# A new step order for fused attention and expert layer, with banks and memory of their own for the last steps of attention

## The chip, the cores and the metric

The kernel runs on one core of one Trainium2 chip. The metric is the device time of one execution in microseconds. Engines are named as in the profile: PE (TensorE, the matrix engine; PEld are its weight loads), ACT (ScalarE), DVE (VectorE), POOL (GpSimd) and SP (SyncE, which only issues transfers). Each engine works through its own instructions in the order in which they were written, and waits on semaphores for the others.

## The reference

Causal attention over 4 batches, 12 heads, 448 positions, 64 wide, and behind it a mixture of 8 experts over the 1792 tokens, each of which goes to one expert:

```python
scores = scale * np.matmul(q, k.transpose(0, 1, 3, 2))       # causal mask, then softmax
attn = np.exp(scores - max); attn = attn / (sum + 1e-09)
x = (attn @ v).transpose(0, 2, 1, 3).reshape(1792, 768)
xn, en = x / (norm(x) + 1e-06), expert_emb / (norm(expert_emb) + 1e-06)
logits = xn @ en.T / tau                                     # (1792, 8)
expert_idx = argmax(logits); gate_w = softmax(logits)[expert_idx]
out[mask] = gate_w * (maximum(x[mask] @ w1[e], 0) @ w2[e])   # w1: 768x1024, w2: 1024x768 per expert
```

## The kernel before

Attention goes by pairs of heads, 24 in all (`NP`), each cut into 4 chunks of 112 query rows. The steps of a pair `p` have short names, and the string `ORDER` (lines 36 to 103) says in which order the steps are issued, `name.pair` by `name.pair`; every instruction of a step joins its engine's queue at that place. The steps the text uses:

- `LD` loads q, k and v of a pair (SP, two transfers, to 4 buffers in turn). `EE` loads the experts' embedding.
- `S0` to `S3` (line 348, PE): the scores of chunk i, 112(i+1) columns, of both heads at once, one head to a bank each. `sp_ring` has two pairs of banks and hands them out in turn: the third score step must wait until the first has been read.
- `Mih` (line 358, DVE) masks the scores of chunk i, head h, and takes the row maximum; `Eih` (line 362, ACT) is the exponential with the row sum.
- `T0`, `T1`, `T20`, `T21`, `T30`, `T31` (line 373, PE) transpose the probabilities by the groups of `GROUPS`, into two banks in turn (`pt_ring`), and `V..` (line 381) copies them out, on ACT ("A") or DVE ("V").
- `PV0` to `PV3` (line 390, PE) are the products with v into the bank `bo`; `VO` (ACT) copies them out. `SA` (POOL) and `RC` (DVE) make the reciprocal of the sums; `X` (PE) and `XE` (DVE) turn and scale the result into rows of x; `WX` writes x to memory.
- Every third pair: `LT` (PE) makes expert logits in the bank `bx`, `LS` (ACT) copies them, `LO` (PE) turns them, `LE` (DVE) scales them. At the end of a batch `R0` to `Rc` choose the expert and rank the tokens (DVE, with `RK` on PE), and `Q0` to `Q3` (ACT) square the rows of x.
- `es0` to `esA`, once: the norm of the experts' embedding. `es1` is a square root on ACT.
- After three batches `Z0` to `Z5` find the most used expert so far, the star. `LW`, `W`, `Wl` load its w1, round it and keep the rest of the rounding (SP, ACT, POOL); `LL`, `Ak`, `Bk` do so with w2 (SP, ACT, DVE), k being one of 8 blocks.
- The end: `XT`, `XH`, `XL` turn and split the first tile of 128 gathered tokens; `F0` to `F5` (PE, line 633) are its product with w1, `RL` (ACT) copies the result, `HT`, `HH`, `HL` turn and split it, `G0` to `G5` are the first six of the eight blocks of its product with w2. `N0` to `Nc` (DVE) and `TB` (PE) make the table of which token goes to which tile, `GA` (POOL) gathers tile 1, `xt`, `xh`, `xl` turn and split it.

Behind `ORDER` come the tiles of the expert layer (`body`, line 822): each has two products (line 633), weights that are loaded when the expert changes, and a scattered write to the output.

Memory is reused: `after` (line 159) gives a buffer a second tile of another type when the first is done with in full. So `aq` (line 175) holds the loaded q and k (`raws`) and the probabilities (`Ps`), and its second tile `aqr` holds the split of the first tile and parts of w2, and may be written only when the last probability has been read. `ar` holds the mask and the logits, and after them `h2[0]`, block 0 of w2.

```python
raws = ring_of(4, P, 2, S, src=aq)                       # line 193
h2 = Parts([part(rr, 0, 0, DM)] + ...)                   # line 221: block 0 of w2 follows the mask and the logits
xh_ring = Ring(part(qr, 0, 0, KD, P), ...)               # line 225
```

Before the first step PE turns the identity 24 times (line 793).

Of the kernel before, what the change touches and what calls it, by code (L numbers as in the profile page):

```python
# [40 lines left out]
PV3.0 E00.2 S2.2 LD.4 SA.1 VO.0 RC.1 S3.2 M20.2 E01.2 E10.2 M21.2 T30.1 E11.2 M30.2 T20.1 E20.2 M31.2 X.0 V30.1 V20.1
S0.3 S1.3 E21.2 XE.0 T21.1 E30.2 T31.1 M00.3 V21.1 E31.2 V31.1 T30.2 E00.3 M01.3 SA.2 T20.2 V30.2 M10.3 S2.3 M11.3 E01.3
V20.2 S3.3 E10.3 M20.3 E11.3 M21.3 PV0.1 E20.3 M30.3 E21.3 M31.3 PV1.1 E30.3 PV2.1 RC.2 PV3.1 E31.3 T0.2 LD.5 T21.2 VO.1
SA.3 S0.4 V21.2 V0.2 S1.4 M00.4 M01.4 T1.2 RC.3 E00.4 T31.2 E01.4 M10.4 X.1 V1.2 M11.4 V31.2 S2.4 E10.4 XE.1 S3.4 E11.4
M20.4 PV0.2 M21.4 E20.4 M30.4 PV1.2 E21.4 M31.4 PV2.2 E30.4 PV3.2 T30.3 LD.6 VO.2 T20.3 E31.4 X.2 V20.3 V30.3 S0.5 XE.2
SA.4 S1.5 T0.3 RC.4 T21.3 V0.3 M00.5 LT.2 M01.5 V21.3 E00.5 E01.5 T1.3 LS.2 T31.3 V1.3 M10.5 LO.2 M11.5 E10.5 T30.4
V31.3 E11.5 S2.5 LE0.2 LE1.2 V30.4 LE2.2 S3.5 M20.5 M21.5 E20.5 PV0.3 M30.5 E21.5 M31.5 PV1.3 E30.5 PV2.3 E31.5 PV3.3
T20.4 LD.7 VO.3 T0.4 V20.4 SA.5 S0.6 V0.4 S1.6 RC.5 M00.6 M01.6 T21.4 E00.6 T1.4 V21.4 E01.6 X.3 V1.4 M10.6 T31.4 M11.6
T30.5 E10.6 XE.3 E11.6 S2.6 V31.4 V30.5 S3.6 M20.6 M21.6 PV0.4 E20.6 M30.6 E21.6 PV1.4 M31.6 E30.6 PV2.4 PV3.4 E31.6
T20.5 LD.8 T0.5 VO.4 V20.5 S0.7 SA.6 V0.5 S1.7 RC.6 M00.7 T21.5 M01.7 E00.7 T1.5 V21.5 E01.7 X.4 V1.5 M10.7 T31.5 M11.7  # L50
E10.7 T30.6 XE.4 E11.7 S2.7 V31.5 V30.6 S3.7 M20.7 M21.7 PV0.5 E20.7 M30.7 E21.7 PV1.5 M31.7 E30.7 PV2.5 PV3.5 E31.7
T20.6 LD.9 T0.6 VO.5 V20.6 SA.7 S0.8 V0.6 S1.8 RC.7 M00.8 M01.8 LT.5 E00.8 E01.8 T21.6 LS.5 T1.6 V21.6 X.5 V1.6 M10.8
T31.6 M11.8 T30.7 E10.8 XE.5 E11.8 S2.8 V31.6 V30.7 WX.5 S3.8 M20.8 Q0.5 M21.8 LO.5 Q1.5 M30.8 T20.7 T0.7 LE0.5 LE1.5
PV0.6 V0.7 LE2.5 V20.7 Q2.5 PV1.6 R0.5 Q3.5 PV2.6 M31.8 PV3.6 R1.5 T21.7 LD.10 VO.6 R2.5 T1.7 V21.7 E20.8 X.6 R3.5 V1.7
T31.7 R4.5 XE.6 E21.8 S0.9 S1.9 R5.5 E30.8 V31.7 T20.8 RK.5 E31.8 R8.5 T30.8 V20.8 PV0.7 R6.5 SA.8 V30.8 R9.5 R7.5 M00.9
# [912 lines left out]
```

## Time and profile before

| | |
|---|---|
| median of 3 runs | 540.91 us (539.68 to 540.98) |
| the profiled execution | 539.1 us, its span (first to last instruction) 537.4 us |
| PE busy in the span | 505.7 us, 94% |
| ACT, DVE, POOL busy | 327.9, 315.2, 70.4 us |
| mean granted clock of PE | 0.97 |

The columns of the profile's views: the timeline has the start from the span's start, the time until the last of the merged instructions ends, engine, line, operation and tiles, the count, and in brackets the idle time before and who ended it. Instructions of one engine overlap a little, so what one costs in a row of equal ones is the distance of their starts, not their duration. The view by windows has, for each stretch, every engine's busy time and count, the granted clock of PE (1.00 is 2.4 GHz, 0.50 is 1.2 GHz), the share of the DMA engines and GB/s.

### The profile page before, as it was taken

The numbers are of one execution on the slowest core, as the hardware profiler recorded it, in microseconds if no ns is written. First come the engines' busy times: TensorE is split into PE (matmuls) and PEld (weight loads), VectorE is DVE, ScalarE is ACT, GpSimd is POOL, SyncE is SP. The second block draws the span as 40 slices with busy tenths as digits, with TensorE's granted clock in tenths as the row PEclk, the third lists the DMA queues.
The fourth block names the chain that finished last, engine by engine and source line by source line (L and its number), as shares of the span: only waits on it lengthen the run. The fifth ranks groups of instructions, "written<-read, shape, count | busy, mean of one in ns | idle before, by whom it ended". The sixth has DMA issues, their size and how long they took to land. (4 is left out here: it accounts for less than half of the span.)

```text
span 537.4 us, 10476 instructions
## 1 busy us (share of the span) xinstructions
PE 505.7 (94%) x3184; PEld 405.3 (75%) x3184; DVE 315.2 (59%) x872; ACT 327.9 (61%) x775; POOL 70.4 (13%) x90
## 2 busy tenths in 40 slices
PE   5899999999999959579999999999999999999994
PEld 4465666665666547568989989998899889988984
DVE  0686787778768827733014698181949362073962
ACT  2998889888988869122125587162939352164861
POOL 2000000000000650023011102121110211010111
PEclk9799999999999979779999999999999999999998
DMA  8032263345226933030153965729495700739551
GB/s 236 7 103 69 91 204 104 105 122 169 72 72 205 362 137 104 1 89 30 60 221 116 404 233 185 263 65 383 166 393 184 267 31 30 295 133 390 177 176 35
DMA packets 27364, 87.16 MB, mean 162 GB/s; under 512 B 2694, under 2 KB 3142, under 8 KB 27280
## 3 DMA queue, kind: packets, MB, share of 16 engines
q1 hardware_dynamic: 24160, 72.38, 38.4%
q0 software_dynamic: 3120, 13.77, 7.3%
q8 instruction: 39, 0.64, 0.5%
q14 instruction: 45, 0.37, 0.2%
HBM read 144.33 MB, written 12.58 MB: 292 GB/s over the span
## 5 line engine op out<-in xcount | busy, mean ns | idle before, releaser
L364 ACT ACTIVATE aq<-aq,mx 112x112 f32<-112x112 f32 (+1 forms) x192 | 99.6, 522 | 10.3 <-DVE mx L359 10.2
L359 DVE CUSTOM_DVE_ANT_0 aq<-bank,ar 112x112 f32<-112x112 f32 (+1 forms) x192 | 76.6, 444 | 16.7 <-PE bank L355 14.0
L379 PE MATMUL bank<-idt,aq 112*112 112x112 f32 x480 | 65.1, 271 | 12.4 <-ACT aq L364 6.4
L379 PEld LDWEIGHTS bank<-idt,aq 112*112 112x112 f32 x480 | 47.7, 136 | 32.2 <-ACT aq L364 14.5
L355 PE MATMUL bank<-aq 64*112 64x112 f32 (+3 forms) x384 | 60.1, 428 | 0.1
L384 DVE COPY ap<-bank 112x336 f32<-112x336 f32 (+1 forms) x72 | 38.9, 543 | 33.5 <-PE bank L379 27.9
L820 DVE TENSOR_TENSOR wl<-fa,wh 128x1024 fp32r<-128x1024 f32 x42 | 48.5, 1223 | 13.2 <-PE bank L638 10.8
L392 PE MATMUL bank<-ap 112*64 112x448 f32 (+3 forms) x384 | 51.8, 409 | 0.0
L662 ACT COPY fa<-bank 128x512 f32<-128x512 f32 x28 | 15.2, 588 | 59.9 <-PE bank L637 51.8
L392 PEld LDWEIGHTS bank<-ap 112*64 112x64 f32 x384 | 26.1, 137 | 29.9 <-issue 19.4
L819 ACT CAST wh<-fa 128x1024 fp32r<-128x1024 f32 x42 | 40.8, 1048 | 11.8 <-PE bank L639 9.6
L703 POOL DMA_INDIRECT out_dram<-fa,isx x18 | 25.1, 1395 | 168.7 <-ACTq L830 40.0
L355 PEld LDWEIGHTS bank<-aq 64*112 64x112 f32 x384 | 27.9, 176 | 12.5 <-issue 0.9
L384 ACT COPY ap<-bank 112x448 f32<-112x448 f32 (+1 forms) x72 | 33.3, 466 | 5.5 <-PE bank L379 5.1
L364 ACT ACTIVATION_READ_ACCUMULATOR aq<-aq,mx 112x1 f32 x192 | 36.5, 190 | 0.0
L543 POOL DMA_INDIRECT fa<-xd,ig x21 | 20.7, 986 | 111.6 <-PE bank L595 78.5
L637 PE MATMUL bank<-wh,aor 128*128 128x512 f32 x84 | 33.8, 402 | 0.0
L638 PE MATMUL bank<-wl,aor 128*128 128x512 f32 x84 | 33.6, 400 | 0.0
L639 PE MATMUL bank<-wh,apr 128*128 128x512 f32 x84 | 33.6, 399 | 0.0
L637 PE MATMUL bank<-wh,aqr 128*128 128x512 f32 x84 | 32.9, 392 | 0.0
L639 PE MATMUL bank<-wh,aqr 128*128 128x512 f32 x84 | 32.8, 391 | 0.0
L638 PE MATMUL bank<-wl,aqr 128*128 128x512 f32 x84 | 32.8, 390 | 0.0
(267 smaller groups left out, 1064.8 us busy)
## 6 DMA issues: line engine op xcount, KB each, us to landing
fa<-in_w_dram SPq DMA_DIRECT2D x76, 768.0 KB
fa<-in_w_dram SPq DMA_DIRECT2D x54, 1024.0 KB
aq<-in_qk_dram SPq DMA_DIRECT2D x24, 448.0 KB
ap<-in_vv_dram SPq DMA_DIRECT2D x24, 224.0 KB
xd<-fa SPq DMA_DIRECT2D x3, 1344.0 KB
fa<-in_w_dram SPq DMA_DIRECT2D x6, 512.0 KB
xd<-fa SPq DMA_DIRECT2D x1, 1120.0 KB
fa<-xd,ig POOLq DMA_INDIRECT x21, 4.7
```

The source lines that it names most:

```text
L355: pe.matmul(sp[h][:CP, :n], raws[p % 4][rows, 0, CP * i : CP * i + CP], raws[p % 4][rows, 1, :n], start=True, stop=True, tile_position=(D ...
L359: v.tensor_tensor_reduce(out=Ps[p % 2][i, h], in0=st.pop(("sp", p, i, h)), in1=mask[i], scale=-0.125, scalar=3e38, op0=ALU.add, op1=ALU.mi ...
L364: ac.activation(x, x, AF.Exp, bias=mxs[p % 3][:, h, i : i + 1], scale=-1.0, accum_out=sums[p % 3][:, h, i : i + 1])
L379: pe.transpose(t[:, x, c], Ps[p % 2][i, h][:, c * CP : c * CP + CP], idt[:CP, :CP])
L384: (ac.copy if q == "A" else v.tensor_copy)(o, st.pop(("pt", p, n)))
L392: pe.matmul(bo[64 * h : 64 * h + 64, CP * c : S], vts[p % 4][:, c, 64 * h : 64 * h + 64], PTs[p % 2][:, h, 4 * c : 3 * c + NC], start=c == ...
L637: pe.matmul(acc[j], xh[:, k], wh[k][:, o], start=k == 0, stop=False)
L638: pe.matmul(acc[j], xh[:, k], wl[k][:, o], start=False, stop=False)
L639: pe.matmul(acc[j], xl[:, k], wh[k][:, o], start=False, stop=k == nk - 1)
L703: g.indirect_dma_start(out=out, out_offset=IndirectOffsetOnAxis(ap=isx[:, t : t + 1], axis=0), in_=ob, in_offset=None, bounds_check=N - 1, ...
L819: ac.copy(h[k], r[:, k])
L820: v.tensor_tensor(l[k], r[:, k], h[k], op=ALU.subtract)
```

## The change

- `ORDER` is another order throughout. The scores of chunks 0 and 2 are now one step (`S02`, 448 columns in one pair of banks), so that a pair takes three turns of `sp_ring`, not four: `S02`, `S3`, `S1`. `es0` stands behind the first exponentials, where it stood ahead of them.
- `T20` and `T21` are copied out by ACT instead of DVE.
- `es1` takes the square root on DVE, 12 small instructions, instead of ACT.
- `end_ring`, the two banks of the second pair of `sp_ring`, serves `XT`, the last `LO`, the last `RK`, `HT` and `TB`; the last `LT` goes to `bo`. Before, the first, fourth and fifth went to `pt_ring`, and the logits and the ranking to `bx`.
- `raws` have a buffer `ak` of their own; the split of the first tile and the blocks 1 and 2 of w2 follow them there.
- Block 0 of w2 comes last for the first tile (`K0`), so that `ORDER` has `G1` to `G6`.
- 16 turns of the identity instead of 24.

```diff
@@ a line of ORDER's first and last part
-LD.0 LD.1 LD.2 EE.0 LD.3 es0.0 es1.0 S0.0 S1.0 M00.0 M01.0 M10.0 S2.0 M11.0 E00.0 S3.0 es2.0 E01.0 M20.0 E10.0 M21.0
+LD.0 LD.1 S02.0 EE.0 LD.2 S3.0 M01.0 M21.0 E01.0 M00.0 M20.0 E21.0 M30.0 S1.0 LD.3 E00.0 M31.0 E20.0 T21.0 T0.0 M11.0
-F4.23 Q3.23 A7.23 F5.23 B7.23 LT.23 RL0.23 RL1.23 HTa.23 LS.23 HTb.23 LO.23 LE0.23 LE1.23 LE2.23 R0.23 R1.23 R2.23 R3.23
+A3.23 X.23 XLb.23 LS.23 F0.23 XE.23 A4.23 B3.23 WX2.23 LO.23 A5.23 F1.23 B4.23 A6.23 LE2.23 LE0.23 A7.23 LE1.23 F2.23
...
+K0 = [1, 2, 3, 4, 5, 6, 7, 0]
-GROUPS = {"0": ((0, 1), 0, "A"), "1": ((0, 1), 1, "A"), "20": ((0,), 2, "V"), "21": ((1,), 2, "V"),
+GROUPS = {"0": ((0, 1), 0, "A"), "1": ((0, 1), 1, "A"), "20": ((0,), 2, "A"), "21": ((1,), 2, "A"),
...
+        end_ring = Ring(*bank[2:4])
...
-        aq, qr = after("aq", 4 * 2 * S + 4 * TRI)
+        ak, kr = after("ak", 4 * 2 * S)
+        aq, qr = after("aq", 5 * DM + F)
...
-        step("es1", FIRST)(lambda p: ac.activation(es[:, 2:3], es[:, 0:1], AF.Sqrt))
+            v.tensor_scalar(guess, es[:, 0:1].bitcast(I32), 1, None, ALU.arith_shift_right)
+            v.tensor_scalar(guess, guess, 532487669.0, None, ALU.add)
+            for _ in range(2):
+                for f in newton(es[:, 2:3], es[:, 0:1], es[:, 2:3], es[:, 3:4]):
+                    f()
...
+            for i in chunks:
+                n = CP * (i + 1)
+                for h in range(2):
+                    st["sp", p, i, h] = o = sp[h][:CP, at : at + n]
+                    pe.matmul(o, raws[p % 4][rows, 0, CP * i : CP * i + CP], raws[p % 4][rows, 1, :n],
+                              start=True, stop=True, tile_position=(D * h, 0), skip_group_check=len(chunks) > 1)
+                at += n
...
+            st["lt"] = bo if p == NP - 1 else bx
+            st["lo"] = t = cut(end_ring.next() if p == NP - 1 else bx, CP, NC, 96)
+            rk = rks[p] = cut(end_ring.next() if p == NP - 1 else bx, CP, NC + 1, E)
-            pt = cut(pt_ring.next(), P, 3, P)
+            pt = cut(end_ring.next(), P, 3, P)
...
-        for _ in range(24):
+        for _ in range(16):
```

Line numbers after the change are up to 20 higher. Three places show what moved. The first is ACT at the start; `fa,es<-fa` is `es0`, `es<-es` behind a table load is the square root, `aq,sum<-aq,mx` is an exponential. Before:

```order
L234 ACT_TABLE_LOAD
L234 ACTIVATE es<-es 8x1
L319 ACTIVATE fa,es<-fa 8x768
L320 ACT_TABLE_LOAD
L320 ACTIVATE es<-es 8x1
L364 ACT_TABLE_LOAD
L364 ACTIVATE aq,sum_139<-aq,mx_136 112x112 x2
```

and now:

```order
L237 ACT_TABLE_LOAD
L237 ACTIVATE es<-es 8x1
L378 ACTIVATE aq,sum_140<-aq,mx_137 112x112
L378 ACTIVATE aq,sum_140<-aq,mx_137 112x336
...
L401 COPY ap<-bank_70 112x3x112
L378 ACTIVATE aq,sum_141<-aq,mx_138 112x112
L322 ACTIVATE fa,es<-fa 8x768
```

The exponentials of the first pair no longer stand behind the embedding's square and the two table loads.

The second place is PE in the middle of attention, one pair from its scores to its next scores; `bank<-aq` or `bank<-ak` are scores, `bank<-ap` the products with v, `bank<-idt,aq` transposes. Before:

```order
L355 MATMUL bank_66<-aq 112x336
L355 MATMUL bank_67<-aq 112x336
L355 MATMUL bank_68<-aq 112x448
L355 MATMUL bank_69<-aq 112x448
L392 MATMUL bank_72<-ap 64x448 x2
L392 MATMUL bank_72<-ap 64x336 x2
L392 MATMUL bank_72<-ap 64x224 x2
L392 MATMUL bank_72<-ap 64x112 x2
```

and now:

```order
L368 MATMUL bank_66<-ak 112x112
L368 MATMUL bank_67<-ak 112x112
L368 MATMUL bank_66<-ak 112x336
L368 MATMUL bank_67<-ak 112x336
L368 MATMUL bank_68<-ak 112x448
L368 MATMUL bank_69<-ak 112x448
L409 MATMUL bank_72<-ap 64x448 x2
L409 MATMUL bank_72<-ap 64x336 x2
L409 MATMUL bank_72<-ap 64x224 x2
L409 MATMUL bank_72<-ap 64x112 x2
```

Chunks 0 and 2 share the banks 66 and 67 in one step; the matrix work is the same.

The third place is ACT from the last `VO` on (`ao<-bank`); `ar<-bank` is the last `LS`, `fa<-bank` the copies `RL`, `L722` and `L742` the casts `Ak`. Before:

```order
L398 COPY ao<-bank_72 128x448
L722 CAST apr<-fa 128x768 x3
L490 ACTIVATE junk,n_114<-fa 112x768 x4
L722 CAST apr<-fa 128x768
L662 COPY fa<-bank_66 128x512
L662 COPY fa<-bank_67 128x512
L431 COPY ar<-bank_73 96x448
```

and now:

```order
L742 CAST akr<-fa 128x768 x2
L415 COPY ao<-bank_72 128x448
L594 CAST akr<-bank_68 128x384
L594 CAST akr<-bank_69 128x384
L742 CAST aqr<-fa 128x768
L449 COPY ar<-bank_72 96x448
L742 CAST apr<-fa 128x768 x4
L509 ACTIVATE junk,n_115<-fa 112x768 x2
L742 CAST arr<-fa 128x768
L509 ACTIVATE junk,n_115<-fa 112x768 x2
L682 COPY fa<-bank_66 128x512
```

The last logits (`LS`) moved from behind the first tile's product to its beginning, and on PE `LT` stands ahead of `F0`, `LO` behind it and `RK` behind `F3`.

## Rows read from the trace of the kernel before

**Rows 1.** Windows: busy us (count) of PE, PEld, DVE, ACT, POOL; clock; DMA.

```profile
10.00:20.00 10.00, 4.07 (x18) 2.50 (x18) 3.40 (x19) 8.28 (x22) 0.00 (x0) 0.68 0.34 91
...
52.00:97.00 45.00, 45.00 (x364) 28.17 (x362) 35.26 (x144) 40.34 (x133) 1.39 (x6) 1.00 0.40 124
...
180.00:200.00 20.00, 14.91 (x105) 10.96 (x106) 8.53 (x30) 14.03 (x35) 14.28 (x7) 0.83 0.65 254
...
230.00:240.00 10.00, 6.55 (x30) 5.42 (x29) 3.27 (x14) 3.64 (x5) 2.94 (x3) 0.77 0.43 120
240.00:250.00 10.00, 10.00 (x58) 8.42 (x57) 2.78 (x9) 1.80 (x4) 3.07 (x4) 0.89 0.00 0
...
237.68:537.40 299.72, 291.11 (x1584) 264.31 (x1584) 154.82 (x231) 144.64 (x224) 43.95 (x38) 0.98 0.52 191
```

**Rows 2.** Timeline of ACT: the step VO of two pairs that follow each other.

```profile
104.00 0.51 ACT L398 COPY ao<-bank 128x448 f32<-128x448 f32 x1
...
111.02 0.51 ACT L398 COPY ao<-bank 128x448 f32<-128x448 f32 x1
```

**Rows 3.** Timeline of PE at the start.

```profile
1.45 5.38 PE L794 MATMUL bank<-idt 128*128 128x128 f32 x24 [1.45 <-POOL idt masks.py:199]
6.76 2.76 PE L355 MATMUL bank<-aq 64*112 64x112 f32 x16
15.94 0.81 PE L379 MATMUL bank<-idt,aq 112*112 112x112 f32 x2 [6.42 <-ACT aq L364]
```

**Rows 4.** Timeline of ACT at the start.

```profile
11.64 0.84 ACT L319 ACTIVATE fa<-fa 8x768 f32<-8x768 f32 x1 [9.32 <-DMA fa<-in_emb_dram]
...
15.40 0.39 ACT L364 ACTIVATE aq<-aq,mx 112x112 f32<-112x112 f32 x1
```

**Rows 5.** Timeline of DVE at the start.

```profile
7.36 0.27 DVE L359 CUSTOM_DVE_ANT_0 aq<-bank,ar 112x112 f32<-112x112 f32 x1 [6.42 <-PE bank L355]
```

**Rows 6.** Groups by line and shape, ACT, 101.57 to 108.58: count, busy us, mean ns.

```profile
L384 ACT COPY ap<-bank 112x448 f32<-112x448 f32 x2 | 1.0, 524 | 0.0
...
L384 ACT COPY ap<-bank 112x224 f32<-112x224 f32 x1 | 0.3, 347 | 0.0
```

**Rows 7.** Timeline of SP: the transfers LW and LL.

```profile
175.38 2.09 SPq L719 DMA_DIRECT2D fa<-in_w_dram  x4
182.43 5.00 SPq L520 DMA_DIRECT2D fa<-in_w_dram  x3
```

**Rows 8.** Timeline of ACT: the fourth cast W.

```profile
191.74 1.04 ACT L521 CAST wh<-fa 128x1024 fp32r<-128x1024 f32 x1 [4.76 <-DMA fa<-in_w_dram]
```

**Rows 9.** Timeline of PE behind it.

```profile
193.27 1.55 PE L379 MATMUL bank<-idt,aq 112*112 112x112 f32 x7 [5.09 <-ACT ap L384]
```

**Rows 10.** Timeline of PE at the end of attention.

```profile
205.69 0.50 PE L637 MATMUL bank<-wh,aqr 128*128 128x512 f32 x1
...
214.54 0.95 PE L428 MATMUL bank<-ao,en 128*32 128x448 f32 x6
...
219.49 0.18 PE L467 MATMUL bank<-O,before 112*112 112x32 f16 x1 [1.81 <-DVE O L458]
...
223.58 0.69 PE L638 MATMUL bank<-aqr,arr 128*128 128x384 f32 x1 [2.85 <-DVE aqr L723]
...
229.98 0.33 PE L637 MATMUL bank<-aqr,arr 128*128 128x384 f32 x1
...
232.41 0.34 PE L639 MATMUL bank<-apr,aqr 128*128 128x384 f32 x1
...
234.61 0.88 PE L573 MATMUL bank<-idt,fa 128*128 128x128 f32 x6 [1.87 <-DMA fa<-xd,ig]
...
237.68 0.77 PE L637 MATMUL bank<-wh,aor 128*128 128x512 f32 x1
```

**Rows 11.** Timeline of DVE: the last instruction of the token table.

```profile
225.72 0.51 DVE L760 TENSOR_TENSOR M<-M,tok 112x336 f16<-112x336 f16 x1
```

**Rows 12.** Timeline of POOL: the gather of tile 1.

```profile
230.51 1.05 POOL L543 DMA_INDIRECT fa<-xd,ig  x1 [28.42 <-DVE us L770]
```

More of the change, by code (lines that the diff above doesn't have):

```diff
@@ L41 @@
[L41 to L55, printed above, removed]
@@ new lines @@
+T20.5 M01.7 E11.6 T30.5 M21.7 V20.5 X.4 M00.7 V30.5 M20.7 T31.5 XE.4 E10.6 T0.6 V31.5 V0.6 S3.7 E30.6 S1.7 M30.7 E00.7
+PV0.5 SA.6 M31.7 E01.7 E20.7 PV1.5 M11.7 E31.7 M10.7 PV2.5 RC.6 PV3.5 E10.7 T1.6 LD.9 VO.5 T21.6 V1.6 LT.5 V21.6 E11.7
+LS.5 T20.6 T30.6 V20.6 X.5 V30.6 T31.6 XE.5 E21.7 T0.7 V31.6 V0.7 S02.8 WX.5 Q0.5 S3.8 M01.8 M21.8 Q1.5 PV0.6 M00.8
+M20.8 Q2.5 M30.8 PV1.6 M31.8 PV2.6 PV3.6 Q3.5 LO.5 T1.7 LE2.5 LD.10 VO.6 LE0.5 T21.7 V1.7 LE1.5 R0.5 S1.8 V21.7 S02.9
+M11.8 E30.7 R1.5 R2.5 T20.7 E31.8 R3.5 SA.7 T30.7 R4.5 V20.7 M10.8 X.6 R5.5 V30.7 T31.7 R8.5 E00.8 M01.9 T31.8 R9.5
@@ L346, in _, with scores @@
             sy.dma_start(vts[p % 4], vv[p])
-        def scores(p, i):
-            n = CP * (i + 1)
+        def scores(p, chunks):
             sp = sp_ring.next()
-            for h in range(2):
-                rows = slice(D * h, D * h + D)
-                st["sp", p, i, h] = sp[h][:CP, :n]
-                pe.matmul(sp[h][:CP, :n], raws[p % 4][rows, 0, CP * i : CP * i + CP], raws[p % 4][rows, 1, :n],
-                          start=True, stop=True, tile_position=(D * h, 0))
+            at = 0
+            for i in chunks:
+                n = CP * (i + 1)
+                for h in range(2):
+                    rows = slice(D * h, D * h + D)
+                    st["sp", p, i, h] = o = sp[h][:CP, at : at + n]
+                    pe.matmul(o, raws[p % 4][rows, 0, CP * i : CP * i + CP], raws[p % 4][rows, 1, :n],
+                              start=True, stop=True, tile_position=(D * h, 0), skip_group_check=len(chunks) > 1)
+                at += n
         def masked(p, i, h):
@@ L367, in attn_moe @@
         for i in range(NC):
-            step(f"S{i}")(lambda p, i=i: scores(p, i))
+            step(f"S{i}")(lambda p, i=i: scores(p, (i,)))
             for h in range(2):
@@ L371, in attn_moe @@
                 step(f"E{i}{h}")(lambda p, i=i, h=h: exps(p, i, h))
+        for two in ((0, 1), (1, 0), (0, 2), (2, 0)):
+            step("S%d%d" % two)(lambda p, two=two: scores(p, two))
         def trans(p, n):
@@ L631, in split_h, with product @@
                    lambda: [low(l[:, o], pt, h[:, o]) for o, pt in pts])
-        def product(acc, xh, xl, wh, wl, ks, nk, w):
+        def product(acc, xh, xl, wh, wl, ks, ends, w):
             for k in ks:
@@ L727, in _ @@
         def _(p):
-            nonlocal pt_ring
             st["acc1"] = bank[0:2]
-            pt_ring = Ring(*bank[2:6])
-            product(st["acc1"], *xs[0][1:], h1, l1, [0], KD, 512)
+            product(st["acc1"], *xs[0][1:], h1, l1, [0], (0, KD - 1), 512)
         for k in range(1, KD):
-            step(f"F{k}", END)(lambda p, k=k: product(st["acc1"], *xs[0][1:], h1, l1, [k], KD, 512))
+            step(f"F{k}", END)(lambda p, k=k: product(st["acc1"], *xs[0][1:], h1, l1, [k], (0, KD - 1), 512))
         for j in range(2):
             step(f"RL{j}", END)(lambda p, j=j: hidden(0, st["acc1"], j))
-        for k in range(GE):
-            step(f"G{k}", END)(lambda p, k=k: product(acc2, *hs[0][1:], h2, l2, [k], KF, 384))
+        for k in K0[:GE]:
+            step(f"G{k}", END)(lambda p, k=k: product(acc2, *hs[0][1:], h2, l2, [k], (K0[0], K0[-1]), 384))
         ni = T("ni", [E], I32)
-        step("N0", END)(lambda p: v.tensor_scalar(ni, rk[:, NC], float(P - 1), None, ALU.add))
+        step("N0", END)(lambda p: v.tensor_scalar(ni, rks[p][:, NC], float(P - 1), None, ALU.add))
         step("N1", END)(lambda p: v.tensor_scalar(ni, ni, 7, None, ALU.arith_shift_right))
@@ L763, in _ @@
         def _(p):
-            st["tb"] = cut(pt_ring.next(), P, 2, NT)
+            st["tb"] = cut(end_ring.next(), P, 2, NT)
             for c in range(NCH):
@@ L799, in attn_moe @@
             f(int(p))
+        pt_ring = Ring(*bank[2:6])
         acc1 = st["acc1"]
```

149 lines of the change are left out of this document (81 added, 68 removed).

## The prediction

> **What bounds the kernel now.** I read the views in this order: the windows, to see in which stretches PE is not busy; the timelines of PE and ACT in those stretches, to see who ends the waits; then the timelines of DVE, POOL and SP behind them. In the middle of attention PE has no gap: 45.00 of 45.00 us, while ACT is busy 40.34 and DVE 35.26 [rows 1]. Two VO in a row lie 7.01 us apart [rows 2], which is the length of a pair without logits; the reader is to see that no engine but PE is full there. From the first product of tile 1 at 237.68 on, PE is busy 291.11 of 299.72 us [rows 1]; the change touches little there. So the time that an order of steps can move lies at three places, where PE is idle or has its clock at 1.2 GHz.
>
> The start: the first scores run at 6.76, then PE waits 6.42 us for an exponential [rows 3]. ACT could have begun it behind the first mask at 7.36 [rows 5], but `es0` and two table loads stand ahead of it, and `es0` waits 9.32 us for the embedding; the first exponential runs at 15.40 [rows 4]. The reader is to see that the transfer, the square and the square root cost nothing by themselves, but through their place in ACT's queue.
>
> The middle stall: SP issued four blocks of w2 at 175.38 and the second three blocks of w1 only at 182.43, behind them [rows 7]. The cast of the fourth w1 block waits 4.76 us for its transfer [rows 8], and a copy that PE needs stands behind that cast: 5.09 us of idle PE [rows 9].
>
> The end of attention: `PV3.23` ends at about 205.7, `LT` comes at 214.54 behind the whole of F, the ranking at 219.49, the first G products wait 2.85 us for the rest of w2's block 0, and tile 1 cannot be turned before its gather has landed at 234.61 [rows 10]. The gather was issued at 230.51 [rows 12], from a token table that is done at 226.2 [rows 11]. From 205.69 to 237.68 are 32.0 us, of which PE's work at 2.4 GHz is some 19 (below).
>
> **The change part by part.** I make the sum against the profiled execution, 539.1 us with a span of 537.4 us; its 1.7 us outside the span stay. The median of the three runs is 540.91, so a time from this sum may stand 1 to 2 us under the new kernel's own median.
>
> *Start.* Lost by PE before: 6.42 us of waiting [rows 3]; in 10 to 20 the clock is 0.68 on average, and all 4.07 busy us of that row lie behind 15.94, at half rate, which loses 2.0 [rows 1]; eight turns of the identity less are 8 x 5.38 / 24 = 1.8 [rows 3]. Together 10.2 us. Lost after: I laid the new order of the first three pairs out by hand with the trace's distances. 16 turns end at 1.45 + 3.6 = 5.05, the first mask comes 0.6 later (7.36 less 6.76), the first exponential at 6.0 to 7.7, depending on when the data are there (they were by 6.76). From then on ACT has no gap until PE is ahead of it. In that layout PE is 1.4 us behind its work when `PV.1` ends, and I add 0.6 for scores at half rate at the beginning: 2.0, within 0.5 and 4.5. The first term is -8.2 (-9.7 to -5.7). The twelve small DVE instructions of the square root lie on DVE while PE works on `PV.0`; uncovered they would be some 2.4 us (at 0.2 each), which the upper end takes in.
>
> *Middle of attention.* PE does the same matmuls, so I take 7.01 us a pair. The new wait is that of the three turns of the score banks: behind a waiting score step stand all transposes and products of PE. Laid out by hand, the masks of `S02` are done more than 2 us before the bank pair comes round, because DVE, which has 9.7 us of 45 free [rows 1], loses two copies a pair. ACT takes them over: a copy of 336 columns is not in ACT's rows, its neighbours are 0.35 us for 224 and 0.52 for 448 [rows 6]; twice a pair, six pairs, that is 4.2 to 6.2 us on 40.34, or 44.5 to 46.6 of 45.0. The distance of starts is nearer to the lower end, since one copy's end overlaps the next one's beginning; I take 0.35 and count nothing, and the other end is a rival below.
>
> *The middle stall.* Lost before: 5.09 us [rows 9], and the clock of 0.83 in 180 to 200 [rows 1], at most 3.4 us, of which about two thirds (2.3, within 1.7 and 3.4) lie behind the idle. After: SP has three blocks of w1, three of w2, then the fourth of w1. With 19 ACT steps between the star and the first cast, and 11 more until the fourth cast, the transfers have about 16 us and the cast is later than its data by some 2 us. What is late next is ACT: from the star to the last `VO` it has some 26.6 us of exponentials, copies and six casts, and PE some 23.5, so that PE loses 3.0 (1.5 to 6). The term is -4.4 (-6.5 to -0.7).
>
> *The end of attention.* Before: 32.0 us [rows 10]. After, by PE's own work: `LT` 0.9, `X` 0.45, F 36 matmuls at 0.23 (8.5 us in all between 205.69 and 214.54, less one `X`) = 8.2, `LO` 0.35, `RK` 0.4, `HT` 0.95, `TB` 0.4, G again 36 matmuls, at (232.41 - 229.98) / 14 = 0.174 from 15 that follow each other [rows 10] = 6.25, `xt` 0.85: 18.8. Waits of PE: 1.0 for the last `VO`, which stands behind two casts; 2.2 between F and G, because `TB` needs the last table step and `HL`; 2.3 from `xt` to the product (3.1 before, partly at half rate). Together 24.3. The chain of the logits runs beside F now: `LT` to ranking took 4.95 [rows 10], ranking to table 226.2 - 219.5 = 6.7 [rows 11], table to landed gather would be 0.4 + 0.5 for `TB` and its copy and 234.6 - 230.5 = 4.1 [rows 12]: 16.7 us behind `LT`, under F and G, though DVE's casts of w2 and `F3` delay it by some 4. So `xt` finds its data, with about 1 us to spare. The term is -7.7; if the chain comes out 3 us later it is -5, if both waits shrink -10. Block 0 of w2 coming last takes the 2.85 us away without a new wait, since its cast then lies under G.
>
> *Clock of the first product.* In 237.68 to 240 and in 240 to 250 PE runs 2.3 and 2.2 us at half rate (0.77 and 0.89 in the windows [rows 1]), which loses 2.2; with PE nearly without gaps ahead of it I take it as gained: -2.2 (0 to -2.3).
>
> Sum: -8.2 - 4.4 - 7.7 - 2.2 = -22.5, so 539.1 - 22.5 = 516.6, rounded to 516.5. All ends together would be 510.6 and 527.7.
>
> **The rivals.** *ACT becomes the bound.* At 0.52 us for each new copy six pairs take 46.6 instead of 45.0; over the 21 pairs behind the start that is 5.6 us: 522. For it speaks that ACT already ends with 4.7 us of 45 free [rows 1], against it that its copies overlap.
>
> *The weights stay late.* If the fourth block of w1 lands as late as before, the stall's term is gone: 521. For it speaks that the same bytes go through one queue; against it the later cast.
>
> *The end is set by the chain, not by banks.* If `LE` to the table is held up by DVE's eight casts, each a wait in front of a chain step, and PE waits for the gather: 2 us gained there instead of 7.7, 522.
>
> *The clock.* Each of the three half-rate stretches cost 2.0 to 2.3 us of work. Two such stretches that stay or arise, at the start and in the gaps between F, G and the first product, give 516.5 + 4.5 = 521. The 24 turns of the identity ahead of the scores took 0.224 us each [rows 3], where the six turns of `xt` at 234.61 took 0.147 [rows 10], so the start is at the lower level. The Trainium skill, TensorE: Matmul & The Clock Gate, section Part 1: The HAM clock gate, says that "the default state is throttled, and activity releases the throttle"; the trace agrees, as PE's long idle at the start and at 188 to 193 is followed by rates of 0.68 and 0.83. By that rule fewer turns of the identity speak against this change.
>
> *Slower.* The three turns of the score banks make PE wait in every pair. The price of one such wait is at least the 0.6 us from a score to its mask [rows 3, 5]. One a pair is 23 x 0.6 = 13.8, 530; two a pair are 27.6, 544, slower than before. It decides from 22.5 / 23 = 1.0 us a pair. Against it stands DVE's free time.
>
> **How the numbers follow.** Forecast 0.45, ACT bound 0.18, late weights 0.10, chain 0.10, clock 0.10, slower 0.05; 0.02 is left for no change. All but the last two are faster by over 0.3% (1.6 us, about what a measurement of this kernel can tell from no change): 0.93, 0.02, 0.05. The forecast's own range is 511 to 522. The whole range, 510 to 527, holds the other faster cases and the ends of the unknown costs, and leaves out the slower ones.
>
> **What would show it.** Right: first exponential by 8 us; VO still 7.0 us apart, with PE at 45 of 45; no wait of a W cast over 1 us; `LT` at once behind `VO.23`, and 23 to 26 us from the last `PV` to the first product of tile 1, which starts near 215. Wrong: gaps of PE in front of score steps, ACT full with PE waiting for its copies, a gather that lands after G, or a clock under 1.00 between 20 and 500. If the product of tile 1 starts near 215 and the time is still over 525, the expert layer has changed, which I take to be the same.

## The result, and the profile after

The changed kernel takes 515.98 us, median of 4 runs (515.45 to 516.11), against 540.29 us for the kernel before in the same comparison (537.85 to 540.98): ratio 0.956, 95% interval 0.952 to 0.959. The forecast was 516.5. The profiled execution has a span of 514.4 us.

I cut both executions into the same six stretches: from the first instructions to `VO.3`, to `VO.15`, to `VO.20`, to `VO.23`, to the first product of tile 1, to the end. The windows of the kernel before (busy us and count of each engine, granted clock of PE, DMA share, GB/s):

```profile
core 0: us, PE busy (x) PEld busy (x) DVE busy (x) ACT busy (x) POOL busy (x), PEclk, DMA share, GB/s
0.80:52.02 51.22, 43.67 (x299) 28.00 (x300) 29.05 (x130) 37.48 (x121) 3.71 (x19) 0.93 0.36 104
52.02:142.00 89.98, 89.98 (x726) 56.33 (x724) 70.57 (x289) 80.57 (x261) 2.78 (x12) 1.00 0.39 124
142.00:176.48 34.48, 34.48 (x281) 21.70 (x280) 27.77 (x116) 29.61 (x95) 0.93 (x4) 1.00 0.45 143
176.48:205.81 29.33, 23.73 (x179) 16.14 (x180) 15.97 (x55) 22.46 (x57) 15.93 (x10) 0.88 0.59 225
205.81:237.68 31.87, 22.69 (x124) 18.84 (x125) 17.05 (x52) 13.11 (x24) 2.94 (x3) 0.86 0.21 59
237.68:537.40 299.72, 291.11 (x1584) 264.31 (x1584) 154.82 (x231) 144.64 (x224) 43.95 (x38) 0.98 0.52 191
```

and of the changed kernel:

```profile
0.80:38.81 38.01, 36.38 (x273) 23.08 (x274) 25.06 (x123) 33.41 (x112) 3.71 (x19) 1.00 0.44 141
38.81:129.18 90.37, 89.83 (x725) 56.97 (x726) 60.98 (x264) 87.37 (x283) 2.74 (x12) 1.00 0.39 123
129.18:166.10 36.92, 36.78 (x297) 23.46 (x297) 26.50 (x118) 35.85 (x115) 0.96 (x5) 1.00 0.43 130
166.10:189.72 23.62, 21.39 (x178) 13.52 (x177) 11.49 (x46) 23.30 (x64) 14.27 (x10) 1.00 0.84 315
189.72:216.63 26.91, 21.54 (x124) 17.83 (x125) 21.20 (x57) 14.54 (x28) 6.32 (x4) 0.94 0.15 43
216.63:514.40 297.77, 288.95 (x1584) 262.75 (x1584) 154.64 (x230) 144.57 (x224) 42.99 (x38) 0.99 0.52 192
```

The first number behind each stretch is its length. Row by row the change is -13.2, +0.4, +2.4, -5.7, -5.0 and -1.9 us, together -23.0, which is the difference of the spans. The +2.4 in the third stretch is no loss: PE is busy throughout in both, and the new order works less far ahead of `VO.3`, so that work left over from the first stretch is done here (the eight turns aside, 18 matmuls fewer in the first stretch and 16 more in the third). The start is therefore -13.2 + 2.4 + 0.4 = -10.4 us up to `VO.20`, the middle's +0.4 included.

The start, first on PE, then on ACT (start, us until the last of the merged instructions ends, and in brackets the wait and who ended it); to be compared with [rows 3, 4]:

```profile
1.44 3.44 PE L812 MATMUL bank<-idt 128*128 128x128 f32 x16 [1.44 <-POOL idt masks.py:199]
4.83 1.77 PE L368 MATMUL bank<-ak 64*112 64x112 f32 x12
7.41 0.64 PE L368 MATMUL bank<-ak 64*112 64x224 f32 x4 [0.80 <-DVE mx L373]
```

```profile
6.33 0.39 ACT L378 ACTIVATE aq<-aq,mx 112x112 f32<-112x112 f32 x1 [4.03 <-DVE mx L373]
...
12.02 0.83 ACT L322 ACTIVATE fa<-fa 8x768 f32<-8x768 f32 x1
```

The first exponential runs at 6.33 instead of 15.40, and the embedding's square at 12.02 finds its data there. PE's 6.42 us of waiting have become 0.80.

The stall [rows 8, 9] is gone: the fourth cast of w1 runs without a bracket at

```profile
181.67 1.05 ACT L540 CAST wh<-fa 128x1024 fp32r<-128x1024 f32 x1
```

What is late there now are ACT's copies, as forecast: it is busy 23.30 of 23.62 us in the fourth stretch. The end on PE, to be compared with [rows 10]:

```profile
187.48 2.11 PE L409 MATMUL bank<-ap 112*64 112x448 f32 x16 [1.12 <-ACT ap L401]
190.33 0.95 PE L446 MATMUL bank<-ao,en 128*32 128x448 f32 x6 [0.73 <-ACT ao L415]
...
193.63 0.50 PE L659 MATMUL bank<-wh,akr 128*128 128x512 f32 x1 [1.31 <-DVE akr L595]
...
205.29 0.56 PE L784 MATMUL bank<-M,turned 112*128 112x42 f16 x16 [1.57 <-DVE aqr L605]
205.69 0.50 PE L657 MATMUL bank<-akr,arr 128*128 128x384 f32 x1
...
213.58 0.82 PE L592 MATMUL bank<-idt,fa 128*128 128x128 f32 x6
215.95 0.40 PE L914 MATMUL bank<-sm,idt 128*128 128x21 f32 x2 [1.55 <-DVE sm L912]
216.63 0.47 PE L657 MATMUL bank<-wh,aor 128*128 128x512 f32 x1 [0.28 <-ACT t L885]
```

The last `PV` ends at 189.59, `LT` follows 0.7 us behind it, where 8.8 us lay between before, and tile 1 is turned at 213.58 without a wait for its gather. From the last `PV` to the first product are 27.0 us, 4.9 less than before and 2.7 more than forecast. Two things in these rows were not in the forecast: the wait of 1.31 us at 193.63 for `XL` (L595), and the clock, which falls as G begins:

```profile
205.89:209.31 3.42, 3.42 (x12) 3.42 (x12) 3.25 (x13) 0.00 (x0) 1.74 (x2) 0.50 0.10 16
```

3.42 us at 1.2 GHz lose 1.7 us. `XL` is late because DVE first has `B1` and `B2` of w2 (L743) to do, and these take 3.97 us where two such subtractions at 208.60 take 1.81:

```profile
189.14 3.97 DVE L743 TENSOR_TENSOR aqr<-fa,akr 128x768 fp32r<-128x768 f32 x2 [3.22 <-ACT akr L742]
193.03 1.01 DVE L595 TENSOR_TENSOR akr<-bank,akr 128x384 fp32r<-128x384 f32 x2
```

### The profile page after: what moved, and what is told of

It is laid out like the page before. It is cut to its first block, busy times and chain, and to the rows that moved or that the text cites. A ratio compares the mean times of both kernels' runs of the same rounds, so it can differ in the third digit from the quotient of the medians.

```text
span 514.4 us, 10514 instructions
## 1 busy us (share of the span) xinstructions
PE 494.9 (96%) x3176; PEld 397.6 (77%) x3176; DVE 299.9 (58%) x836; ACT 339.0 (66%) x820; POOL 71.2 (14%) x90
## 5 line engine op out<-in xcount | busy, mean ns | idle before, releaser
L378 ACT ACTIVATE aq<-aq,mx 112x112 f32<-112x112 f32 (+3 forms) x192 | 99.7, 524 | 4.0 <-DVE mx L373 4.0
L396 PE MATMUL bank<-idt,aq 112*112 112x112 f32 x480 | 62.6, 265 | 1.6 <-ACT ap L401 0.8
L368 PE MATMUL bank<-ak 64*112 64x112 f32 (+3 forms) x384 | 56.2, 416 | 0.8 <-DVE mx L373 0.8
L401 ACT COPY ap<-bank 112x336 f32<-112x336 f32 (+2 forms) x120 | 51.2, 458 | 3.0 <-PE bank L396 1.1
L562 POOL DMA_INDIRECT fa<-xd,ig x21 | 22.4, 1066 | 105.4 <-PE bank L614 77.5
L368 PEld LDWEIGHTS bank<-ak 64*112 64x112 f32 x384 | 27.0, 173 | 12.8 <-issue 3.1
L659 PE MATMUL bank<-wh,akr 128*128 128x512 f32 x84 | 32.9, 392 | 1.3 <-DVE akr L595 1.3
L657 PE MATMUL bank<-wh,akr 128*128 128x512 f32 x84 | 33.0, 392 | 0.0
L658 PE MATMUL bank<-wl,akr 128*128 128x512 f32 x84 | 32.8, 390 | 0.0
L416 POOL TENSOR_SCALAR sum<-sum 112x8 f32<-112x8 f32 x24 | 5.6, 232 | 151.8 <-ACT aq L378 115.8
```

What stands on the lines that cost most here:

```text
L368: pe.matmul(o, raws[p % 4][rows, 0, CP * i : CP * i + CP], raws[p % 4][rows, 1, :n], start=True, stop=True, tile_position=(D * h, 0), skip ...
L378: ac.activation(x, x, AF.Exp, bias=mxs[p % 3][:, h, i : i + 1], scale=-1.0, accum_out=sums[p % 3][:, h, i : i + 1])
L396: pe.transpose(t[:, x, c], Ps[p % 2][i, h][:, c * CP : c * CP + CP], idt[:CP, :CP])
L401: (ac.copy if q == "A" else v.tensor_copy)(o, st.pop(("pt", p, n)))
L657: pe.matmul(acc[j], xh[:, k], wh[k][:, o], start=k == ends[0], stop=False)
L658: pe.matmul(acc[j], xh[:, k], wl[k][:, o], start=False, stop=False)
```

## The experiments

In the diffs of `ORDER` only the moved names are shown; times are medians, with the ratio to the kernel before and its 95% interval. For the changed kernel these are 515.98 and 0.956 (0.952 to 0.959).

**The start alone, in the kernel before**

```diff
-LD.0 LD.1 LD.2 EE.0 LD.3 es0.0 es1.0 S0.0 ...
+LD.0 LD.1 LD.2 EE.0 LD.3 S0.0 ... E31.0 es0.0 ... es1.0 es2.0 es3.0 es4.0 es5.0
...
-es1: ac.activation(es[:, 2:3], es[:, 0:1], AF.Sqrt)
+es1: the 12 instructions on DVE
```

> The kernel before with one part of the change: the embedding's square stands behind the first pair's exponentials, and its square root is 12 small instructions on DVE; 24 turns of the identity, four score steps a pair and everything else stay as before. Theory (the start was lost through the place of the square and the two table loads in ACT's queue): first exponential at 8 to 9 us instead of 15.40, PE's wait of 6.42 us under 1.5, the half-rate stretch at 13.59 gone, and 531 to 534 us against 540.3, 6.4 us of it from the start term without its 1.8 for the identity. Rival (the start was won by the new order of scores and by fewer turns of the identity): 537 to 540.

535.08 us against 539.04 for the kernel before beside it, 0.992 (0.989 to 0.995): between the two readings. The first exponential runs at 7.61, and `VO.3` comes 4.8 us earlier. The view of the waits for PE up to 52 us shows a new one, and the windows a new stretch at half rate behind it:

```profile
PE bank L344 <- DVE fa L337: 2.0, 1, 2.0
```

```profile
20.00:25.00 5.00, 5.00 (x31) 3.05 (x31) 2.67 (x14) 2.74 (x10) 0.00 (x0) 0.66 0.43 126
```

L344 is `es9`, the turn of the embedding, which the old order has too early for a square that comes later: PE waits 2.0 us for `es8` (L337), and a clock of 0.66 over 5 us loses 1.7. So I estimate the place in ACT's queue at 4.8 + 2.0 + 1.7 = 8.5 us in the old order, if everything that hangs on the square moves with it. Nearly half of that was given back here by one step left where it was.

**The square put back, in the changed kernel**

```diff
-S02.0 EE.0 LD.2 S3.0 ... M31.1 es0.0 T30.0 ... V1.0 es1.0 V30.0
+S02.0 EE.0 LD.2 es0.0 es1.0 S3.0 ...          (es1 on ACT again)
```

> The changed kernel with the embedding's square and its square root (on ACT, with its table loads) put back ahead of the first exponential. Theory (place in ACT's queue): the first exponential moves from 6.33 to about 15, PE waits 6 us or more there and falls to half rate, 523 to 527 us against 516.0. Rival (the order of the scores carries the start): below 519.

522.80 us, 0.970 (0.968 to 0.973), just under the theory's range. The embedding comes earlier than expected, so that the first exponential runs at 12.25, not at 15, and PE waits for it 4.47 us, not 6; its clock is 0.82 from 10 to 15 and 0.84 from 15 to 20:

```profile
13.34 1.19 PE L388 MATMUL bank<-idt,aq 112*112 112x112 f32 x5 [4.47 <-ACT aq L370]
```

`VO.3` comes 6.8 us later than in the changed kernel (45.57 against 38.81): the order of the scores, with the square in front, keeps none of these 6.8 us. That the time is also 6.8 us more is chance. Behind `VO.3` the stretches differ by -3.2 to +1.6 us and cancel: the fifth, with the same order of the end, takes 23.76 us instead of 26.91, as PE does not wait for `XL` there and its clock stays full.

```profile
197.82:221.58 23.76, 19.75 (x125) 16.33 (x125) 19.61 (x57) 14.42 (x27) 4.70 (x4) 1.00 0.17 47
```

**Copies of T20 and T21 on DVE again**

```diff
-GROUPS = {... "20": ((0,), 2, "A"), "21": ((1,), 2, "A"),
+GROUPS = {... "20": ((0,), 2, "V"), "21": ((1,), 2, "V"),
```

> The changed kernel with the copies of T20 and T21 on DVE, as before the change. ACT then has about 40.3 us of 45 in six pairs instead of 43.6. Theory (the copies cost nothing in the middle of attention, only from 160 us on, where ACT is busy 19.48 of 20 us and PE waits 2.8 us in all): VO.3 to VO.9 45.0 to 45.3, PE's waits between 160 and 190 us shrink to about 1, total 514 to 516 against 516.0. Rival 1 (ACT is the bound in the middle too): six pairs come down from 45.27 to 44.98, total 512 to 514. Rival 2 (the copies had to leave DVE, so that masks are done before the score banks come round): PE waits before score steps, six pairs at 46 or more, total 518 to 522.

519.31 us (517.67 to 524.05), 0.966 (0.962 to 0.969): slower than the changed kernel, the intervals do not touch. The time is that of the second rival, its mechanism is not: PE waits for no score bank. Six pairs take 45.68 instead of 45.27 us, and the weight loads of the transposes wait more for exponentials and copies, here from `VO.3` to `VO.9`, first in this run, then in the changed kernel:

```profile
PEld bank L396 <- ACT aq L378: 2.7, 5, 0.7
PEld bank L396 <- DVE ap L401: 1.0, 4, 0.4
...
PEld bank L396 <- ACT ap L401: 0.4, 1, 0.4
```

```profile
PEld bank L396 <- ACT ap L401: 1.1, 2, 0.7
...
PEld bank L396 <- ACT aq L378: 0.7, 1, 0.7
```

That is 4.1 us in these rows (in all, times, longest) against 1.8. The end, by contrast, is shorter here than in the changed kernel, at full clock:

```profile
191.98:217.53 25.55, 20.02 (x125) 16.30 (x125) 21.40 (x57) 14.53 (x28) 7.38 (x4) 1.00 0.17 51
```

My theory that the copies are free on either engine falls. The profiled execution of this run is its fastest; where the others lose up to 6 us more, no trace shows.

**24 turns of the identity**

```diff
-        for _ in range(16):
+        for _ in range(24):
```

> The changed kernel with 24 turns of the identity instead of 16. Theory (PE is what the start waits for, so each turn costs its own time): eight more turns at 0.11 (full rate, granted from 4.51 on) to 0.22 us, that is 0.9 to 1.8 us, 516.9 to 517.8 against 516.0. Rival 1 (the first data or ACT set the start): 516.0, no change. Rival 2 (sixteen turns leave the clock low later on): a half-rate stretch that is there now would be gone, and the time lower than 516.0; the trace of the changed kernel shows none between 4.51 and 205.89.

518.23 us, 0.962 (0.959 to 0.964). The turns end 1.94 us later, and so does all behind them:

```profile
1.44 5.38 PE L812 MATMUL bank<-idt 128*128 128x128 f32 x24 [1.44 <-POOL idt masks.py:199]
6.75 1.90 PE L368 MATMUL bank<-ak 64*112 64x112 f32 x12
9.46 0.64 PE L368 MATMUL bank<-ak 64*112 64x224 f32 x4 [0.81 <-DVE mx L373]
```

`VO.3` stands at 40.87, 2.06 later, `VO.23` at 191.78, 2.06 later. Eight turns cost 2.06 us, 0.26 each, a little above the 0.9 to 1.8 that were expected, and none of it is made up. The view gives the clock 1.00 from the start in both, though the turns take 0.22 us each, so it does not show the rate of that stretch. The first scores do: with 16 turns the first twelve take 1.77 us, as later ones of the same step do (at 8.59 and 12.71).

**The end's banks as before**

```diff
-            st["lt"] = bo if p == NP - 1 else bx
+            st["lt"] = bx
...          LO and RK in bx, XT, HT and TB on pt_ring
```

> The changed kernel with the banks of the last steps as before: the last LT, LO and RK in the bank of X, and XT, HT and TB on the ring of the probabilities' transposes, from F0 on with four banks. Order and memory as changed. Theory (the banks carry part of the end's gain): the last X must wait for the copy of the logits (1.2 us from LT's end), LO for XE, G1 for the ranking's reader, together 1.5 to 3 us, so VO.23 as now and the first product of tile 1 at 28.5 to 30 us behind the last PV instead of 27.1; 517.5 to 519 us against 516.0. Rival (the order alone carries it): 27 us behind the last PV and 516, or up to 0.4 us less, since TB then no longer waits for the bank of HT.

In this order `LS` stands behind `X`, which now has the same bank: the logits of the last three pairs are not the reference's, the last tokens go to other tiles, and the waits that the theory speaks of do not arise. Its 514.91 us, 0.956 (0.953 to 0.959), therefore decide nothing on the logits' bank. One thing can be read: with four banks in the ring `TB` waited 0.97 us instead of 1.57, for the last table step (M, L780).

**The memory as before**

```diff
-        ak, kr = after("ak", 4 * 2 * S)
-        aq, qr = after("aq", 5 * DM + F)
+        aq, qr = after("aq", 4 * 2 * S + 4 * TRI)
```

> The changed kernel with the loaded q and k back in one buffer with the probabilities, so that the split of the first tile and the blocks 1 to 3 of w2 may be written only when the last probability has been read. Theory (the last transposes end at 186.4 us and the first such write starts at 188.26, so nothing waits): 516, within 0.7. Rival (the memory is what lets the end start early): the casts and the split wait, the first product of tile 1 is 1 to 3 us later, 517 to 519.

516.14 us, 0.959 (0.955 to 0.962), and 26.89 us from `VO.23` to the first product against 26.91: the theory holds. The memory of its own gains nothing in this order, since the last probability is read before the first such write would start.

**Scores of chunks 0 and 2 apart**

```diff
-S02.p
+S0.p S2.p
```

> The changed kernel with the scores of chunks 0 and 2 in two steps behind each other (four turns of the two pairs of banks for a pair of heads, as before the change), in the changed order. Theory (in this order a fourth turn is waited for: S3 needs the masks of chunk 0, which stand on DVE behind those it had not to wait for): a wait of 0.2 to 0.7 us a pair, VO.3 to VO.9 at 46.3 to 49 us instead of 45.27, 520 to 530 us. Rival (the merged step saves nothing in the middle, as PE is full there): 45.3 us and 516 to 517.

Here `S3` stands ahead of the masks of chunk 0 and takes their bank, so these masks read other scores and the tiles are filled otherwise; only the times within attention are comparable, and the wait that the theory speaks of does not arise. 529.29 us, 0.983 (0.980 to 0.987); six pairs take 46.86 us, of which PE is idle 1.14. A fourth turn costs 1.6 us in six pairs even so. What it costs in an order with the masks in their place was not tried.

**The end in another order**

```diff
-PV1 A1 PV2 A2 Wl5 PV3 B1 VO XHa B2 LT XHb XLa A3 X XLb LS F0 XE
+PV1 XHa XHb A1 XLa XLb PV2 Wl5 PV3 B1 VO A2 LT A3 X LS F0 XE B2
...
-HTb HHa HHb Na Nb Nc HLa TB HLb U0 U1 G1 IG GA IU IS ... G5 G6
+HTb HHa HLa Na Nb HHb HLb Nc U0 U1 G1 U2 U3 G2 TB IG GA IU IS U4 U5 B0 ... G5 HV G6 NT
```

`HV` (L911 to L915, the row of halves) and `NT` (the number of tiles) stood behind `ORDER` until now, ahead of tile 1's product.

> The changed kernel with its end in another order: XH and XL ahead of the casts of w2's blocks 1 and 2; HL ahead of the table steps and TB behind G2; the row of halves and the load of the number of tiles, which stand ahead of tile 1's first product on PE, between G5 and the end of G. Theory (the end is set by PE's own waits, 1.31 us for XL, 1.57 for HL and TB, 1.55 and 0.28 ahead of the product): some 3.5 us less, the first product of tile 1 at 23 to 24 us behind the last PV instead of 27.1, 512 to 513 us against 516.0. Rival 1 (the chain from the logits to the gather sets the end): the turn of tile 1 waits for its gather, 514 to 516. Rival 2 (the half-rate stretch at G only moves): 513 to 515.

516.38 us, 0.958 (0.955 to 0.961): no gain. The waits of 1.31, 1.57, 1.55 and 0.28 us are gone but for 0.49 ahead of `HV`, and G ends 2.6 us earlier. But PE now waits for the gather, as the first rival has it. The next rows show that it is not the chain of the logits that makes the gather late. PE, then POOL, then DVE:

```profile
213.16 1.54 PE L592 MATMUL bank<-idt,fa 128*128 128x128 f32 x6 [2.05 <-DMA fa<-xd,ig]
```

```profile
206.85 3.52 POOL L562 DMA_INDIRECT fa<-xd,ig  x1 [15.27 <-DVE mt L809]
```

```profile
206.74 0.94 DVE L743 TENSOR_TENSOR aqr<-fa,arr 128x768 fp32r<-128x768 f32 x1
207.60 1.81 DVE L743 TENSOR_TENSOR apr<-fa,apr 128x768 fp32r<-128x768 f32 x2
```

The gather occupies POOL for 3.52 us instead of 1.06, until 0.96 us after DVE's three subtractions end at 209.41. PE waits 2.05 us for it and then has the clock at 0.69 from 211.0 to 216.5, as the second rival has it. In the profiled execution the first product comes 2.2 us sooner behind `VO.23` (24.75 us), and the stretch behind it takes 298.9 us instead of 297.8.

The changed kernel shows the same hold-up, where it does no harm. Its first gather began at 207.26, ahead of the three subtractions (207.74 to 210.41); its second began among them and took 2.62 us:

```profile
207.26 1.06 POOL L562 DMA_INDIRECT fa<-xd,ig  x1 [15.84 <-DVE ef L799]
208.62 2.62 POOL L562 DMA_INDIRECT fa<-xd,ig  x1 [0.30 <-issue]
```

```profile
208.60 1.81 DVE L743 TENSOR_TENSOR apr<-fa,apr 128x768 fp32r<-128x768 f32 x2
```

**The same, with the subtractions behind the gather**

```diff
+... Nb HHb Nc HLb G1 TB IG GA IU IS U0 U1 U2 U3 U4 U5 B6 G2 G3 G4 G5 HV B0 B7 G6 NT
```

> The end reordered as in the run before it (XH and XL ahead of the casts of w2, the first HL ahead of the table, halves and number of tiles ahead of the end of G), and besides: TB behind G1, its index copy first on DVE, and the big subtractions B0 and B7 of w2 behind the gather's issue (B6 between). In the run before, the gather of tile 1 took POOL 3.52 us from 206.85, until the three subtractions on DVE were done at 209.41, against 1.06 in the changed kernel, and PE waited 2.05 us for it and fell to half rate. Theory (DVE's subtractions hold the gather's issue up, and nothing else sets the end): the gather takes POOL about 1 us, lands by 211, PE waits under 0.5 us for it, no half-rate stretch follows, the first product of tile 1 is 22 to 23 us behind the last PV (27.1 in the changed kernel), and 510 to 512 us against 516.0. Rival 1 (the gather takes 3.5 us whatever DVE does): as the run before, 515 to 516.5. Rival 2 (what is gained ahead of tile 1 is lost in the expert layer, where weights are then late): first product as early, but 514 to 516.

511.53 us, 0.949 (0.946 to 0.951): better than both kernels, 4.4 us below the changed one, whose interval lies apart. The gather, and the windows from `VO.23` to the first product and from there to the end:

```profile
206.30 1.06 POOL L562 DMA_INDIRECT fa<-xd,ig  x1 [14.55 <-DVE le L795]
```

```profile
190.04:211.78 21.74, 20.26 (x124) 16.29 (x124) 19.39 (x54) 12.61 (x24) 3.71 (x3) 1.00 0.16 46
211.78:509.60 297.82, 289.17 (x1584) 262.72 (x1584) 155.66 (x232) 146.47 (x227) 44.00 (x39) 1.00 0.53 193
```

PE is idle 1.5 of 21.74 us, against 5.4 of 26.91, and its clock is full. The expected 22 to 23 us behind the last `PV` are 21.9. The expert layer takes 297.8 as in the changed kernel, so nothing is given back. `TB` and smaller steps moved too, so the 4.9 us between the last two runs are not the subtractions' alone; that they held the gather up is shown by the gather's own time.

**The fourth load of w2 ahead of the fourth of w1**

```diff
-LW3.17 ... LL3.23
+LL3.23 LW3.17
```

> The changed kernel with the fourth load of w2 (1.5 MB in two blocks of 768 KB, or 768 KB in one) issued ahead of the fourth block of w1, as before the change; nothing else moves. Theory (the stall in the middle was made by the order of the loads in one queue): at the 250 GB/s of that stretch the fourth cast of w1 waits some 3 us for its data, ACT and then PE stand still, VO.23 is 1.5 to 4 us later than 189.72, 517.5 to 520 us against 516.0. Rival (the later cast alone cures it): the data are there at 181.67 all the same, 516.

516.35 us, 0.957 (0.954 to 0.960), and `VO.20` to `VO.23` in 23.87 us against 23.62: the rival. The data of the fourth w1 block are there in time in either order of the loads; here its load is issued at 176.81, 11.4 us behind the first of w2 (7.1 in the kernel before), and the cast at 182.21 has no wait. What is left is that ACT asks for the data later: 18.2 us behind the first load of w1 in the changed kernel, 13.2 in the kernel before, where they were there after 18.0. No run moved the cast back.

**A bank of its own for TB**

```diff
-            st["tb"] = cut(end_ring.next(), P, 2, NT)
+            st["tb"] = cut(bank[4], P, 2, NT)
```

> The changed kernel with the token table TB in a bank that no HT uses, so that it need not wait until the first HL has read it. Theory (TB's wait of 1.57 us was half for the bank): the wait is 0.9 to 1.0 us, what remains is for the last table step on DVE; the gather is issued 0.6 us earlier, 514.5 to 516 us against 516.0, the lower end if the half-rate stretch of 3.4 us in G goes as well. Rival (G1 needs the same HL, so that nothing is won): 516, with the wait moved from TB to G1.

515.32 us, 0.956 (0.954 to 0.959). `TB` waits 1.0 us instead of 1.57, as the theory has it, but the time can't be told from the changed kernel's. The profiled execution has stretches at half rate where the changed kernel has none, as

```profile
190.00:195.00 5.00, 4.38 (x18) 2.35 (x15) 5.00 (x6) 4.35 (x8) 1.33 (x1) 0.50 0.02 5
```

so one execution can't weigh 0.6 us.

**The last pairs' copies on DVE, on top of the better end**

```diff
-            (ac.copy if q == "A" else v.tensor_copy)(o, ...)
+            (ac.copy if q == "A" and (n[0] != "2" or p < 20) else v.tensor_copy)(o, ...)
```

> The reordered end of the run that took 511.5 us, and the copies of T20 and T21 of the last four pairs on DVE instead of ACT, where ACT is busy 23.3 of 23.6 us and DVE 11.9 (VO.20 to VO.23). Theory (ACT bounds the last pairs): PE's wait of 1.1 us for a copy ahead of the last PV and of 0.5 ahead of a transpose shrink, VO.20 to VO.23 takes 22.6 to 23.0 us instead of 23.63, and 510.5 to 511.2 us. Rival (the casts of w1 fill what the copies leave free, or DVE's masks come late): 23.6 us and 511.5 to 512.

512.03 us, 0.949 (0.947 to 0.951): no gain, the rival's time. `VO.20` to `VO.23` shrinks from 23.63 to 22.95 us as expected, but `VO.19` to `VO.20` grows from 5.80 to 6.12 and `VO.23` to the first product from 21.74 to 22.07. What is gained in the one stretch is lost in those on both sides.

## Why the prediction was right, and where it was not

The time came out within 0.6 us of the forecast. The places and the causes of the loss were the right ones, but that closeness is luck: errors of 1 to 3 us in the terms cancelled, the start and the middle stall gaining 3.5 us more than forecast and the end 2.7 less.

*Start*, forecast -8.2, measured -10.4 (up to `VO.20`) and outside its own bounds. The place of the square is shown by the run that puts it back (6.8 us), and by the run in the old order (estimated 8.5 with what hangs on it); the identity's 1.8 by the run with 24 turns (2.06). These two make 8.9; the other 1.5 us no run attributes. The step that was mis-sized is "lost after: 2.0": from the first turn to `VO.3` PE is idle 1.0 us (38.01 less 36.38 less 0.64 ahead of the first turn), and the half-rate scores that the forecast had added did not come. Up to `VO.20` PE's idle time fell by 5.2 us (7.55 to 2.31), which the forecast had at 5.0 (6.42 less 1.4). Its busy time fell by 5.1, which the forecast had at 3.2 (2.0 and 1.8, less 0.6); of these 1.9 about 1 us stays unexplained.

*Middle of attention*, forecast 0, measured +0.4 over twelve pairs (counted in the 10.4), about right. ACT is busy 87.37 of 90.37 us, that is 43.7 in six pairs, below the 44.5 and 46.6 of the forecast, so ACT as the bound did not come about. The sign "VO still 7.0 us apart" was badly chosen: the order repeats after six pairs. In the changed kernel neighbours lie 8.4, 7.3 and 7.7 us apart behind 84.08, and in the kernel before, where 7.01 was read, they lie up to 10.2 us apart (86.84 to 96.99). Six pairs, 45.27 us against 44.97, are the measure. What the merged scores contribute no run shows.

*Middle stall*, forecast -4.4, measured -5.7. PE is idle 2.2 us (23.62 less 21.39) instead of 3.0, and before it had lost 7.9 instead of 7.4: 5.60 of idle time and 2.3 in the clock. The forecast named the order of SP's loads and the later cast. The order of the fourth blocks is worth nothing (the run with w2 ahead of w1); the later cast is what is left, by elimination.

*End of attention*, forecast -7.7, measured -5.0. The step that failed is the list of PE's waits. Those it named came out 1.0 us shorter than the forecast's 5.5: 0.73 for the last `VO` (1.0 forecast), 1.57 between F and G (2.2) and 2.2 from 214.4 to the product (2.3). It lacked the 1.31 us for `XL` and the 1.7 us of G at half rate, and PE's own work took some 0.7 more than 18.8. 24.3 - 1.0 + 1.3 + 1.7 + 0.7 = 27.0. Other runs with the same order of the end bear this out. With copies on DVE, where the wait for `XL` came and the half rate did not, the fifth stretch took 25.55 us instead of 26.91; with the square put back, where neither came, 23.76. The claim that the chain of the logits is hidden held: at the 4.1 us from issue to landing of [rows 10, 12] the gather issued at 207.26 is there at 211.4 by estimate, 2 us ahead of the turn at 213.58. What the banks add beside the order, which the forecast left together, remains open; the memory adds nothing.

*Clock of the first product*, forecast -2.2, measured -1.9, as the last stretch went from 299.7 to 297.8 us; from 216.63 to 225 the clock is now 1.00.

Of the rivals, the clock came true in part, with one stretch of 3.4 us. That was also one of the signs of being wrong, as was ACT full with PE waiting for its copy (1.12 us at 187.48); and 27.0 us to the product lie outside the 23 to 26. The rule that the prediction took from the Trainium skill, TensorE: Matmul & The Clock Gate, Part 1: The HAM clock gate, was set against fewer turns of the identity; the run with 24 turns shows no harm from 16. The wait for score banks occurs once, 0.80 us at 7.41, and not in every pair.

## What to carry to other kernels

A one-time computation that is not urgent costs through its place in an engine's queue, and moving it pays only when its readers on the other engines move too. When PE's waits at the end of a stage have been taken away one by one and the time stays, look at what the next transfer was waiting for: here it was not its data but a few large subtractions on another engine. Sum a forecast by stretches and compare it by stretches, because a total can be right with two wrong terms.
